# Half-batch 4's k and q: transposed by DMA instead of by TensorE, in a fused attention and SwiGLU kernel

## The chip, the cores and the metric

The kernel runs on one core of a Trainium2 chip. The metric is the device time of one execution in microseconds (us), as the median of several runs. The engines are named as in the profile: PE is TensorE (PEld its weight loads), DVE is VectorE, ACT is ScalarE, POOL is GpSimd, and SP is SyncE, which here only issues transfers.

## The reference

Eight batches of eight heads of causal attention over 576 positions with head size 64, with a bias from a running sum of a score `s`; its output, laid out as 4608 tokens by 512, goes through a SwiGLU block with 1536 hidden channels.

```python
scores = (q @ k.transpose(0, 1, 3, 2)) / np.sqrt(D)
cum = np.cumsum(np.maximum(s, 0.0), axis=-1)
bias = np.minimum(-(cum[:, :, :, None] - cum[:, :, None, :]), 0.0)
scores = np.where(causal, -1e9, scores + bias)
attn = softmax(scores)                       # over the last axis
x = (attn @ v).transpose(0, 2, 1, 3).reshape(B * S, H * D)
g = x @ w_gate
out = (g * sigmoid(g) * (x @ w_val)) @ w_out
```

All inputs and the output are float32; the matrix products inside the kernel are in bfloat16.

## The kernel before

**Units of work.** A half-batch is four heads. There are 16, numbered 0 to 15, and 64 heads, numbered `kk` from 0 to 63; half-batch `h` is `kk // 4` and the head within it is `step`. Before a half-batch can be scored its k and q have to stand transposed (head dimension on the partitions) in one of two buffers, `KQ[hb % 2]`, which has one tile for each pair of rows `r` (0 and 1). Heads with `step` 0 and 1 read the tile of r = 0, heads with `step` 2 and 3 the tile of r = 1.

**The way of k and q.** `load_qk` (L140) brings a half-batch in float32 from DRAM, 576 KB for k and 576 KB for q. `cast_one` makes bfloat16 of them in the tiles `ck` and `cq` (on POOL at L246, later on ACT at L244). From there two ways lead to `KQ`:

- By TensorE: `pe_transpose` (L287) transposes nine 128 by 128 blocks of k and nine of q through the identity matrix into PSUM, in groups of five and four, and `pe_out` copies each group out of PSUM twice, once for each r (ACT at L314 for k, DVE at L316 for q). `prep_one` issues one group; the table `PREP_AT` says when.
- By DMA: `scratch` (L260) writes `ck` and `cq` to DRAM (tiles `ks`, `qs`, 288 KB each), `transposes` (L270) reads them back with a transposing DMA into `pk` and `pq`, and `split` (L274) copies them into `KQ` on DVE, four copies for a half-batch. `scratch` and `transposes` are issued on SP.

The constant `NPE` is the number of half-batches that go by TensorE: 5, so half-batches 0 to 4. Half-batches 5 to 15 go by DMA. `aug` (L183) adds the rows of the bias to `KQ`.

**The order of the work is written out by hand** and the engines follow it, each in its own order. After a start-up part (heads 0 to 7), a generator `attn_items` yields the attention work in pieces, and the loop at the end of the kernel weaves it between the pieces of the SwiGLU block, token tile by token tile (nine tiles of 512 tokens). One head is scored in four pieces (`score_piece`, `ci` 0 to 3, L359 on PE, the exponential at L369 on ACT, masks at L374 and L379 on POOL). `av_piece` (L396) multiplies with V into a PSUM bank, and `av_out` normalises it on DVE (L412, L413) and so frees the bank. For heads 0 to 15 a pair of heads is then transposed by TensorE (`x_pe`, L445) and copied into `XT` on DVE (L452). `XT` is what the gate and value products (L629) read; their results pass ACT (L650) and DVE (L652, L663), and the last product is at L686 or L735.

While half-batch 3 (heads 12 to 15) is scored, the first token tile is in its last product (L686), which holds four of the eight PSUM banks. The other four pass among score pieces, V products and transposes. `take` gives out the bank that was released longest ago, so the bank of every product is fixed when the program is built.

**What else is issued there.** `side` issues loads at given places of the scoring. V of batch 1 is cast on POOL at heads 11 and 12 (L168), and then the five loads of V of batch 2 are issued on SP (`load_v`, L157) into the same buffer; that V is cast on POOL when half-batch 4 is scored. k and q of half-batch 5 are loaded in start-up. Calls of `split` do not run at once: they are put on a list, `later`, and `do_later(1)` takes one of them at places of the loop; in the first token tile past n = 30 it takes none:

```python
if tt == 0 and n > 30:
    pass
elif i >= 2 * NFT or i % (2 if tt == 1 else 4) == 1:
    do_later(1)
```

Whatever of a half-batch is left on the list is taken before its first head is scored.

**SP** works through its list of transfers in order. An instruction that has to wait (for a cast, for the scratch write that a transposing DMA reads, for a free buffer) holds up all that stand behind it. Each transfer also reuses one of eight semaphores in turn, and so waits until the transfer that stands eight places ahead of it has landed.

Of the kernel before, what the change touches and what calls it, by code (L numbers as in the profile page):

```python
# [19 lines left out]
def kernel(  # L20
# [14 lines left out]
    B, H, S, D = q.shape  # L35
# [6 lines left out]
    NHB = BH // HB  # L42
    NR = HB // 2
# [33 lines left out]
        tc.tile_pool(name="dram", bufs=1, space=bass.MemoryType.DRAM)  # L77
    )

    NPE = 5  # L80
    XB = 2
    KS = {i: dram.tile([NR * S, 128], BF16, name=f"ks{i}") for i in range(NPE, NHB)}
    XS = {
        i: dram.tile([NCH * 128, 128], BF16, name=f"xs{i}") for i in range(XB * H // 2, BH // 2)
    }
    QS = {i: dram.tile([NR * S, 128], BF16, name=f"qs{i}") for i in range(NPE, NHB)}

# [16 lines left out]
    first = first_sbuf.enter_context(tc.tile_pool(name="first", bufs=1))  # L104
# [5 lines left out]
    with tc.manual_schedule():  # L110
# [36 lines left out]
        def load_qk(hb):  # L147
            load_one(hb, "k")
            load_one(hb, "q")

        def load_v(b, cs, eng=nc.sync):
            if 0 in cs:
                loaded["v", b] = raw.tile([128, NCH, H, D], FP32, tag="rawv", bufs=1, name="rawv")
            t = loaded["v", b]
            for c in cs:
                n = 128 if c < 4 else TAIL
                eng.dma_start(  # L157
                    t[0:n, c, :, :],
                    v[b, :, c * 128 : c * 128 + n, :].rearrange("h p d -> p h d"),
                )  # L160
# [97 lines left out]
        def scratch(hb):  # L258
            for name, SC in (("k", KS), ("q", QS)):
                nc.sync.dma_start(  # L260
                    SC[hb].rearrange("(x j) c -> x (j c)", j=J),
                    cts[name, hb].rearrange("x j r d -> x (j r d)"),
                )
# [3 lines left out]
        def transposes(hb):  # L267
            for name, SC in (("k", KS), ("q", QS)):
                prs[name, hb] = cp.tile([128, NR * S], BF16, tag="p" + name, bufs=1, name="p" + name)
                nc.sync.dma_start_transpose(prs[name, hb], SC[hb])  # L270
# [184 lines left out]
        later = []  # L455

        def do_later(n):
            while n > 0 and later:
                f, *args = later.pop(0)
                f(*args)  # L460
                n -= 1
# [5 lines left out]
        def side(h, step, ci):  # L467
            bh = HB * h + step
            for c in V1_AT.get((bh, ci), ()):
                cast_v(1, c, nc.gpsimd)  # L470
            if bh == H + 4 and ci == 3:
                load_v(2, range(5))
            if h == 4 and (step, ci) in ((0, 1), (2, 1)):
                load_qk(6 + step // 2)
            if h >= 5 and h + 3 < NHB and (step, ci) == (0, 1):
                load_qk(h + 3)
            hb = h + 1
            if NPE <= hb < NHB:
                late = hb == NPE
                if late and (step, ci) == (0, 1):  # L480
                    scratch(hb)
                if late and (step, ci) == (0, 3):
                    transposes(hb)
                if (step, ci) == (0, 1):
                    aug(hb, GP4)
                first = 1 if hb < NPE + 3 else 0
                if step in (first, first + 1) and ci == (3 if late else 1):
                    for r in range(NR):
                        later.append((split, hb, "kq"[step - first], r))
            hb = h + 2  # L490
            if hb == NPE and step == 3 and ci % 2 == 1:
                cast_one(hb, "kq"[ci // 2], nc.gpsimd)
            if NPE < hb < NHB:
                six = hb == NPE + 1
                if (step, ci) == ((2, 0) if six else (0, 2)):
                    cast_one(hb, "k", nc.scalar)
                if (step, ci) == ((2, 2) if six else (1, 2)):
                    cast_one(hb, "q", nc.scalar)
                if (step, ci) == ((3, 0) if six else (2, 0)):
                    scratch(hb)  # L500
                if (step, ci) == (3, 3 if six else 0):
                    do_later(NR * 2)
                    transposes(hb)
            if ci != 1:
                return
            bn = h // 2 + 1
            if 3 <= bn < B:
                if h % 2 == 0:
                    if step == 2:
                        load_v(bn, (0, 1))  # L510
                    if step == 3:
                        load_v(bn, (2, 3, 4))
# [4 lines left out]
        def side_v(h, step, ci):  # L517
            bn = h // 2 + 1
            if h == 4 and (step, ci) in V2_AT:
                cast_v(2, V2_AT[step, ci], nc.gpsimd)  # L520
            if 3 <= bn < B and h % 2 == 1 and (step, ci) in V_AT:
                cast_v(bn, V_AT[step, ci], nc.scalar)
# [3 lines left out]
        def prep_one(hb, i, eng=None):  # L526
# [7 lines left out]

        PREP_AT = {
            2: {(1, 2): 0, (2, 0): 2, (2, 2): 1, (3, 0): 3},
            3: {(1, 3): 0, (2, 1): 1, (2, 3): 2, (3, 1): 3},
        }

        AV_AT = {  # L540
# [6 lines left out]
        def attn_items():  # L547
            for kk in range(H, BH + 2):
                h, step = divmod(kk, HB)
                if kk < BH:  # L550
                    if step == 0:
                        do_later(NR * 2)
                    if step == 1 and 3 < h + 1 < NPE:
                        cast_one(h + 1, "k", nc.gpsimd)
                        cast_one(h + 1, "q", nc.gpsimd)
                    if step == 2 and 3 < h + 1 < NPE:
                        aug(h + 1, GP4)
                    for ci in range(4):
                        score_piece(kk, ci)
                        side(h, step, ci)  # L560
                        side_v(h, step, ci)
                        yield kk + 0.1 + ci / 8
                        if (step, ci) in PREP_AT.get(h, ()):
                            prep_one(
                                h + 1, PREP_AT[h][step, ci],
                                (nc.scalar, nc.vector)[ci // 2] if h == 2 else None,
                            )
                            yield kk + 0.1 + ci / 8
                for x in X_AT.get(kk, (kk - 2,)):
                    if x % 2 == 1 and H <= x < BH:  # L570
                        if x < XB * H:
                            x_pe(x // 2)
                            yield kk + 0.5
                        else:
                            x_in(x // 2)
                for p in AV_AT.get(kk, (kk - 1,)):
                    if H <= p < BH:
                        av_piece(p, (0, 1, 2))
                        yield kk + 0.6
                        av_piece(p, (3,))  # L580
                        yield kk + 0.7
                        av_piece(p, (4,))
                        av_out(p)
                        if p >= XB * H and p % 2 == 1:
                            x_out(p // 2)
                        yield kk + 0.8
# [369 lines left out]
        aug(3, SP4)  # L956
        load_v(1, range(5))
        load_qk(4)
        load_qk(5)
        x_pe(0, nc.vector)  # L960
        values(4, 5)
        x_pe(1, nc.scalar)
# [40 lines left out]
        for tt in range(NTT):  # L1003
            lo = H * (tt + 1) + LAGS[tt]
            hi = min(H * (tt + 2) + LAGS[tt + 1], BH + 2)
            span = 36 if tt < FIRST7 else 34.5
            if hi == BH + 2:
                span = 30
            n0 = 5 if tt == 0 else 0
            n = 0  # L1010
            todo = {FIRST7 - 1: W_SUMS, FIRST7: W_DIFFS}.get(tt, [])
            if tt == FIRST7:
                for _ in range(3):
                    weight_op(*todo.pop(0))
            for i, cost in enumerate(ffn_items(tt)):
                n += cost
                if todo and (i >= 24 if tt < FIRST7 else i % 2 == 1):
                    weight_op(*todo.pop(0))
                if tt == 0 and n > 30:
                    pass  # L1020
                elif i >= 2 * NFT or i % (2 if tt == 1 else 4) == 1:
                    do_later(1)
                if seconds:
                    seconds.pop(0)()
                for f in hook.pop(n, ()):
                    f()
                done = min(1.0, max(0, n - n0) / (span - n0))
                if tt == 0:
                    done = (
                        0.57 * max(0, n - n0) / (24 - n0) if n < 24  # L1030
                        else min(1.0, 0.57 + 0.43 * (n - 24) / (span - 24))
                    )
                pump(lo + (hi - lo) * done)
# [31 lines left out]
```

## Time and profile before

| what | value |
|---|---|
| median of 3 runs | 376.75 us (376.2 to 377.3) |
| the profiled execution | 375.79 us, of which the span from first to last instruction is 374.0 us |
| PE busy | 360.7 us, 96% of the span |
| DVE, ACT, POOL busy | 289.6 us (77%), 240.4 us (64%), 212.3 us (57%) |
| granted TensorE clock | 0.999 |
| DMA moved | 64.23 MB, mean 172 GB/s |
| SP's queue (hardware dynamic) | 84976 packets, 41.46 MB, 45.2% of 16 engines' span |
| POOL's queue (software dynamic) | 12128 packets, 22.21 MB, 22.6% |

The span counts from the first to the last instruction of the profiled execution; the time counts 1.79 us more that lie around it. All times of day below, such as "at 66.62", are microseconds from the start of that span. A row of the timeline gives start, duration, engine, line, operation, tiles written and read, shapes and how many instructions were merged; in brackets stands the idle time before it and what ended that. Matmuls are pipelined, so a row's duration reaches past the start of the next row on PE: what a group of matmuls costs is the distance between the starts.

### The profile page before, as it was taken

The numbers are of one execution on the slowest core, as the hardware profiler recorded it, in microseconds if no ns is written. First come the engines' busy times: TensorE is split into PE (matmuls) and PEld (weight loads), VectorE is DVE, ScalarE is ACT, GpSimd is POOL, SyncE is SP. The second block draws the span as 40 slices with busy tenths as digits, with TensorE's granted clock in tenths as the row PEclk, the third lists the DMA queues.
The fourth block names the chain that finished last, engine by engine and source line by source line (L and its number), as shares of the span: only waits on it lengthen the run. The fifth ranks groups of instructions, "written<-read, shape, count | busy, mean of one in ns | idle before, by whom it ended". The sixth has DMA issues, their size and how long they took to land.

```text
span 374.0 us, 8759 instructions
## 1 busy us (share of the span) xinstructions
PE 360.7 (96%) x3259; PEld 230.6 (62%) x3300; DVE 289.6 (77%) x578; ACT 240.4 (64%) x471; POOL 212.3 (57%) x325
## 2 busy tenths in 40 slices
PE   7799899999999999999999999999999999999995
PEld 6584456655555556855685559655865585476464
DVE  8968776468995899588967997699858867975984
ACT  8777677698876877588757875686566523323321
POOL 8883555856455647494649464955675516315320
PEclk9999999999999999999999999999999999999999
DMA  7899999799877997896779675984132103002003
GB/s 239 193 258 253 219 257 267 237 303 247 245 186 220 254 262 196 178 281 205 211 167 266 178 182 174 255 206 98 40 119 62 35 19 128 2 0 95 20 0 114
DMA packets 97146, 64.23 MB, mean 172 GB/s; under 512 B 77232, under 2 KB 82736, under 8 KB 97104
## 3 DMA queue, kind: packets, MB, share of 16 engines
q1 hardware_dynamic: 84976, 41.46, 45.2%
q0 software_dynamic: 12128, 22.21, 22.6%
q8 instruction: 26, 0.43, 0.5%
q14 instruction: 16, 0.13, 0.1%
HBM read 37.90 MB, written 19.86 MB: 154 GB/s over the span
## 4 chain that ended last, share of the span: by engine, by line
PE 85%; DMA 6%; POOL 5%; ACT 1%; issue 1%; DVE 1%; DVEq 0%; POOLq 0%; ACTq 0%
PE bank L629 45%; PE bank L735 17%; PE bank L359 10%; PE bank L396 7%; PE bank L686 5%; DMA rawk<-in_k_dram 4%; DMA rawv<-in_v_dram 2%; POOL rawv L157 1%; POOL vt L168 1%; POOL wv L332 1%; ACT pt L369 1%; PE bank L287 0%; POOL rawq L140 0%; ACT kq L314 0%; POOL kq L211 0%
## 5 line engine op out<-in xcount | busy, mean ns | idle before, releaser
L369 ACT ACTIVATE pt<-bank 128x512 bf16<-128x512 f32 (+1 forms) x256 | 120.4, 510 | 31.0 <-PE bank L359 18.2
L629 PE MATMUL bank<-XT,wg 128*128 128x512 bf16 x418 | 110.3, 379 | 1.2 <-DVE pp L652 0.3
L629 PE MATMUL bank<-XT,wv 128*128 128x512 bf16 x412 | 109.3, 379 | 1.1
L650 ACT ACTIVATE th<-bank 128x512 bf16<-128x512 f32 x108 | 64.7, 599 | 55.9 <-PE bank L629 53.6
L652 DVE SCALAR_TENSOR_TENSOR pp<-th,bank 128x512 bf16<-128x512 bf16 x108 | 73.6, 682 | 19.2 <-ACT th L650 18.7
L663 DVE SCALAR_TENSOR_TENSOR ht<-pp,bank 128x512 bf16<-128x512 bf16 x108 | 74.1, 686 | 10.6 <-PE bank L629 0.4
L359 PE MATMUL bank<-kq 128*128 128x128 bf16 (+4 forms) x576 | 75.6, 240 | 1.5 <-DMA kq<-HL 1.0
L672 POOL TENSOR_TENSOR ht<-ht 128x512 bf16<-128x512 bf16 x35 | 40.4, 1154 | 52.2 <-DVE su L670 52.1
L359 PEld LDWEIGHTS <-kq 128*128 128x128 bf16 x576 | 45.8, 98 | 31.5 <-issue 1.9
L629 PEld LDWEIGHTS <-wv 128*128 128x128 bf16 x432 | 38.4, 98 | 36.5 <-issue 0.6
L629 PEld LDWEIGHTS <-wg 128*128 128x128 bf16 x432 | 38.3, 98 | 34.2 <-issue 0.7
L396 PEld LDWEIGHTS <-pt 128*128 128x128 bf16 x960 | 41.9, 98 | 17.2
L374 POOL TENSOR_SCALAR_AFFINE_SELECT pt<-pt 128x512 bf16<-128x512 bf16 x56 | 36.8, 658 | 27.3 <-ACT pt L369 22.7
L396 PE MATMUL bank<-vt,pt 128*128 128x65 bf16 x960 | 47.0, 194 | 0.4 <-POOL vt L168 0.3
L430 POOL DMA_DIRECT2D xs<-ot x24 | 21.7, 905 | 30.0 <-DVE ot L413 27.6
L735 PEld LDWEIGHTS <-ht 128*128 128x128 bf16 x336 | 31.2, 98 | 4.3
L413 DVE TENSOR_TENSOR ot<-bank,rc 128x320 bf16<-128x320 f32 x64 | 31.5, 492 | 2.2
L183 POOL DMA_DIRECT2D kq<-HL x48 | 28.9, 604 | 0.0
L735 PEld LDWEIGHTS <-su 128*128 128x128 bf16 x252 | 23.5, 98 | 3.3
L686 PE MATMUL bank<-wo,ht 128*128 128x512 bf16 x90 | 24.8, 379 | 0.3
L800 POOL TENSOR_TENSOR ysb<-ysb 128x512 f32<-128x512 f32 x12 | 15.2, 1270 | 15.3 <-DVE ysb L794 15.3
L379 POOL TENSOR_SCALAR_AFFINE_SELECT pt<-pt 128x64 bf16<-128x64 bf16 x56 | 14.8, 264 | 15.8 <-ACT pt L369 15.7
(93 smaller groups left out, 384.6 us busy)
## 6 DMA issues: line engine op xcount, KB each, us to landing
out_dram<-ysb POOLq DMA_DIRECT2D x32, 256.0 KB, 4.5
rawv<-in_v_dram SPq DMA_DIRECT2D x28, 256.0 KB
rawk<-in_k_dram SPq DMA_DIRECT2D x12, 576.0 KB
rawq<-in_q_dram SPq DMA_DIRECT2D x12, 576.0 KB
xs<-ot POOLq DMA_DIRECT2D x24, 160.0 KB, 3.5
ks<-ck SPq DMA_DIRECT2D x11, 288.0 KB
qs<-cq SPq DMA_DIRECT2D x11, 288.0 KB
rawk<-in_k_dram POOLq DMA_DIRECT2D x3, 576.0 KB, 7.3
```

The costliest lines, as they stand in the source:

```text
L359: nc.tensor.matmul(sc[:, o : o + w], T[:, 1, e * S + 128 * tj : e * S + 128 * (tj + 1)], T[:, 0, e * S + lo : e * S + hi], start=not maske ...
L369: nc.scalar.activation(pt[:, c0 : c0 + n], sc, AF.Exp, scale=0.125)
L374: nc.gpsimd.affine_select(pt[:, 1088:1600], pt[:, 1088:1600], pattern=[[0, 4], [1, 128]], compare_op=ALU.is_ge, fill=zreg, base=0, channel ...
L396: nc.tensor.matmul(av[:, bi * (D + 1) : (bi + 1) * (D + 1)], pt[:, c0 : c0 + 128], VT[b % 2][:, tj, h, :], start=(tj == 0), stop=(tj == bi),)
L413: nc.vector.tensor_mul(ot[:, :, e * D : (e + 1) * D], av3[:, :, 0:D], rc[:, :, None].to_broadcast([128, NCH, D]),)
L629: nc.tensor.matmul(view(bs, TT), w[:, c, f0 : f0 + 128], xt[:, c, :], start=(c == 0), stop=(c == 3),)
L650: nc.scalar.activation(th, pg, AF.Tanh, scale=0.5)
L652: nc.vector.scalar_tensor_tensor(pp, in0=th, scalar=1.0, in1=pg, op0=ALU.add, op1=ALU.mult)
L663: nc.vector.scalar_tensor_tensor(hp[:, 2 * k2 : 2 * k2 + 2, :].rearrange("p a n -> p (a n)"), in0=pp, scalar=0.5, in1=pv, op0=ALU.mult, op ...
L672: (nc.vector if ft == NFT - 1 else nc.gpsimd).tensor_sub(hp[:, 1:3, :], hp[:, 1:4:2, :], hp[:, 0:3:2, :])
L686: nc.tensor.matmul(view(pys[ts_], DM), hps[ft // 2][:, 2 * (ft % 2) + half, c0 : c0 + 128], WO[j][:, ft % WKO, :], start=(ft == 0), stop=( ...
L735: nc.tensor.matmul(ps, lhs(p), rhs(p), start=(first and p == 0), stop=(last and p == NP - 1), skip_group_check=True,)
```

## The change

Half-batch 4 goes by DMA instead of by TensorE. `NPE` becomes 4, and a new constant `NSC` (5) keeps the places of half-batches 5 and later. While half-batch 3 is scored, `scratch(4)` is placed after the last piece of step 1, `transposes(4)` and the five loads of V of batch 2 after the first piece of step 2, and the four calls of `split` go on the list `later` after the last piece of step 2 (k) and the second piece of step 3 (q). In the first token tile past n = 30 the list is now worked off where its head belongs to half-batch 4. The loads of k and q of half-batch 5 move in the program from start-up to the last score piece of head 12. The casts of half-batch 4 stay on POOL, at their place.

```diff
-    NPE = 5
+    NPE = 4
+    NSC = 5
...
-            if bh == H + 4 and ci == 3:
-                load_v(2, range(5))
+            if h == 3:
+                if (step, ci) == (1, 3):
+                    scratch(4)
+                if (step, ci) == (2, 0):
+                    transposes(4)
+                    load_v(2, range(5))
+                if (step, ci) in ((2, 3), (3, 1)):
+                    for r in range(NR):
+                        later.append((split, 4, "kq"[step - 2], r))
+                if (step, ci) == (0, 3):
+                    load_qk(5)
...
         PREP_AT = {
             2: {(1, 2): 0, (2, 0): 2, (2, 2): 1, (3, 0): 3},
-            3: {(1, 3): 0, (2, 1): 1, (2, 3): 2, (3, 1): 3},
         }
...
-                    if step == 1 and 3 < h + 1 < NPE:
+                    if step == 1 and h == 3:
                         cast_one(h + 1, "k", nc.gpsimd)
                         cast_one(h + 1, "q", nc.gpsimd)
-                    if step == 2 and 3 < h + 1 < NPE:
+                    if step == 2 and h == 3:
                         aug(h + 1, GP4)
...
         load_qk(4)
-        load_qk(5)
...
                 if tt == 0 and n > 30:
-                    pass
+                    if later and later[0][1] == 4:
+                        do_later(1)
```

In the lines left out `NPE` is replaced by `NSC` in `side`, where the places of half-batches 5 and later are worked out.

More of the change, by code (lines that the diff above doesn't have):

```diff
@@ L477, in side @@
             hb = h + 1
-            if NPE <= hb < NHB:
-                late = hb == NPE
+            if NSC <= hb < NHB:
+                late = hb == NSC
                 if late and (step, ci) == (0, 1):
@@ L485, in side @@
                     aug(hb, GP4)
-                first = 1 if hb < NPE + 3 else 0
+                first = 1 if hb < NSC + 3 else 0
                 if step in (first, first + 1) and ci == (3 if late else 1):
@@ L490, in side @@
             hb = h + 2
-            if hb == NPE and step == 3 and ci % 2 == 1:
+            if hb == NSC and step == 3 and ci % 2 == 1:
                 cast_one(hb, "kq"[ci // 2], nc.gpsimd)
-            if NPE < hb < NHB:
-                six = hb == NPE + 1
+            if NSC < hb < NHB:
+                six = hb == NSC + 1
                 if (step, ci) == ((2, 0) if six else (0, 2)):
```

## The prediction

> **What bounds the kernel now.** I read the chain of waits first.
>
> ```profile
> PE 85%; DMA 6%; POOL 5%; ACT 1%; issue 1%; DVE 1%; DVEq 0%; POOLq 0%; ACTq 0%
> ```
>
> PE sets the time, and outside start-up it hardly rests, so a microsecond taken from PE's queue or put into it as a wait moves the end by a microsecond. Then the timeline of PE where half-batch 3 is scored.
>
> ```profile
> 57.58 0.44 PE L287 MATMUL bank<-ident,ck 128*128 128x128 bf16 x5
> 57.86 0.44 PE L445 MATMUL bank<-ident,ot 128*128 128x128 bf16 x5
> ...
> 61.43 0.44 PE L287 MATMUL bank<-ident,cq 128*128 128x128 bf16 x5
> 61.71 0.38 PE L359 MATMUL bank<-kq 128*128 128x320 bf16 x2
> ...
> 66.40 0.39 PE L287 MATMUL bank<-ident,cq 128*128 128x128 bf16 x4
> 66.62 0.38 PE L359 MATMUL bank<-kq 128*128 128x320 bf16 x2
> ...
> 68.90 0.39 PE L359 MATMUL bank<-kq 128*128 128x128 bf16 x4
> ```
>
> No row has idle time before it. The L287 rows are the transposes that go away; the row at 68.90 is the first of half-batch 4's scores, the deadline of its k and q. Third, SP's timeline.
>
> ```profile
> 54.18 9.56 SPq L157 DMA_DIRECT2D rawv<-in_v_dram  x5
> 63.85 0.55 SPq L140 DMA_DIRECT2D rawk<-in_k_dram  x1
> 64.50 0.42 SPq L140 DMA_DIRECT2D rawq<-in_q_dram  x1
> 68.21 0.36 SPq L260 DMA_DIRECT2D ks<-ck  x1
> 69.49 0.35 SPq L260 DMA_DIRECT2D qs<-cq  x1
> 71.14 1.74 SPq L270 DMA_TRANSPOSE pk<-ks  x1
> 72.98 1.29 SPq L270 DMA_TRANSPOSE pq<-qs  x1
> ```
>
> That is half-batch 5's way by DMA, the model for half-batch 4's. Its landings, from the trace's semaphore records: ks 71.1, qs 72.0, pk 75.6, pq 77.5; ahead of them k of 5 at 59.8, q of 5 at 61.6, V of batch 2 from 62.4 to 66.8, k and q of 6 at 68.7 and 70.3. Last, DVE's timeline, which shows when the copies out of pk are due.
>
> ```profile
> 63.60 0.46 DVE L452 COPY XT<-bank 128x576 bf16<-128x576 bf16 x1
> 64.47 0.20 DVE L412 RECIPROCAL rc<-bank 128x5 f32<-128x5 f32 x1 [0.41 <-PE bank L396]
> 64.70 0.49 DVE L413 TENSOR_TENSOR ot<-bank,rc 128x320 bf16<-128x320 f32 x1
> ...
> 79.58 0.45 DVE L274 COPY kq<-pk 64x1152 bf16<-64x1152 bf16 x1
> 79.95 0.67 DVE L652 SCALAR_TENSOR_TENSOR pp<-th,bank 128x512 bf16<-128x512 bf16 x1
> ```
>
> Half-batch 5's first copy runs at 79.58, 4.0 us after pk landed. Keep that margin in mind.
>
> **What goes away.** 18 transposes on PE. By the distance of starts the four groups take 0.28 (57.58 to 57.86), 0.28 (61.43 to 61.71), 0.23 (62.60 to 62.83) and 0.22 (66.40 to 66.62): 1.01 us, all on the path. Four ACT copies (1.51 + 1.47 us) and four DVE copies (1.66 + 1.46) go too; PE waited for none of them, so they are worth nothing. Added on DVE are four splits of 0.45 to 0.95 us, less than what leaves it: nothing by themselves, but for their waits.
>
> **What does not move.** The loads of half-batch 5 change place in the program, but the order of the built instructions shows them in the same place on SP, straight behind those of 4, with the same waits. SP does not wait for PE, so they start at 45.59 as before: nothing. The casts of 4 keep their place on POOL (54.30 and 56.88, the second held by the landing of q of 4 at 56.8).
>
> **The new chain, step by step.** SP issues the scratch writes behind the casts, at 55.4 and 58.0. Their data stand behind k and q of 5 in the same rings. In the row of before a scratch write landed 0.8 us after the load ahead of it (70.3 to 71.1), so ks of 4 lands at 61.6 + 0.8 = 62.4 and qs 0.9 later. SP waits for ks, issues pk (1.74 us) and then pq. The latency from issue to landing was 4.4 us for pk of 5 and 4.5 for pq: pk lands at 66.8, pq, issued at 64.3, at 68.8. Over all 22 such transposes the latency was 3.0 to 7.9 us, the long ones with loads of V ahead; I take 4.4, since here too only small transfers stand ahead. The earliest is 61.6 + 3.0 = 64.6, the latest I allow 62.4 + 6.4 = 68.8, 6.4 being that of pk of 6.
>
> [...]
>
> **The first wait.** By the order of DVE's instructions the first split of k stands behind the XT copy of heads 10 and 11 (63.60) and ahead of the normalising of heads 12 and 13 (64.47, 65.51). DVE gets there at 63.0, since its old copies are gone and PE is earlier, and stands still until 66.8. Then 0.45 for the split and 0.62 for the normalising (64.47 to about 65.1): head 12's V bank is free at 67.9. PE needs that bank for the third score piece of head 15; before, that was the row at 66.62, now due at 66.62 - 1.01 = 65.6. So PE waits 2.3 us. Behind it the second split and head 13's normalising (69.0) feed the fourth piece and the transposes of heads 12 and 13 and cost about 0.1 more; q's first split, after pq at 68.8, is done at 69.5, ahead of the first scores of half-batch 4 at about 70.3 against 68.90 before. Net of the 1.01 saved, +1.4. PE loses nothing here if pk lands by 64.4, and breaks even at about 65.4.
>
> **The second wait.** The five V loads now stand behind pq on SP and are issued from 65.6 instead of 54.18. Everything behind keeps its distance, but now starts from pq's landing (68.8) and not from that of q of 5 (61.6): 7.2 us later. V of batch 2 lands at 69.6 to 74.0, and POOL casts it from 74.38 + 1.4: in time. k and q of 6 land at 75.9 and 77.5; ACT casts them at 76.51 + 1.4 and 79.75 + 1.4: in time, by 2 us. ks of 5 lands at 78.3, pk of 5 is issued then and lands at 82.8 with 4.4 to 4.5. DVE wants it at 79.58 + 1.4 = 81.0. The margin of 4.0 us is used up and DVE waits 1.8. There DVE runs with hardly a gap, and PE's next uses of the banks that DVE frees have little room (the V bank normalised by about 83.9 is taken by the value product at 84.07), so all but 0.2 reaches PE: +1.6. pq of 5 lands at 84.7, due 87.4: in time. At half-batch 6 pk landed 0.5 us before its copy (93.3 and 93.77). SP was idle for 3.7 us before (75.50 to 79.17), so that much of the 7.2 is absorbed; 3.5 remains against a slip of 3.0: just in time, 0 to 0.3.
>
> **Sum.** -1.01 + 2.4 + 1.6 = +3.0. From the profiled execution, 374.0 of span and 1.79 around it, that is 375.79 + 3.0 = 378.8; the median of the runs lies 0.96 above that execution, so 376.75 + 3.0, about 379.7. With pk of 4 at 65.9 to 68.5 and the queue moving with it, the likeliest case alone gives 377.9 to 381.9.
>
> **Rivals.** *No wait (chance 0.2).* The rings drain faster without V in them, ks lands with q of 5 and pk takes 3.0: landing at 64.6, pq soon after, and half-batch 5 then moves by some 5 us, pk landing at about 79.4. PE keeps nearly all of its 1.01 us: 375.8. For it: the shortest latencies in the profile (3.0, 3.1). Against: those have nothing ahead of them in the queue. It decides at pk of 4 by 64.4 and pk of 5 by 79.8. *First wait only (0.15).* pk of 4 late, but V and the loads of 6 go faster in a queue with no tail of 5 in it, so that pk of 5 lands by 81: 376.75 + 1.4 = 378.1, with an early pk 377.3. *The delay runs on (0.1).* Output stores on POOL's queue (256 KB each, four issued from 73.14 to 79.07) now share the engines with the scratch writes of 5; at the 6.4 us latency pk of 5 lands at 84.7 or later, half-batch 6 and the XT transposes behind it are late as well: +5 to +7, 382 to 384. The forecast holds 0.55.
>
> A run tells about 0.3% (1.1 us) from no change: 375.6 to 377.9 is "same". The no-wait rival lies near the lower edge and gives 0.1 faster, 0.1 same; the first-wait rival gives 0.05 same, 0.1 slower; the rest is slower. The range runs from the no-wait rival's time to the likeliest case's upper end: 375.7 to 381.9, leaving out faster runs below it and most of the running-on case.
>
> **What would show it.** In the changed kernel's profile: no L287 rows near 58 to 67; the loads of 5 still issued at about 45.6; DVE idle 3 to 4 us ahead of an L274 row near 66.8, released by pk; PE idle about 2 us before a score piece, released by DVE's normalising; V of batch 2 issued from about 65.6; a second idle time of DVE ahead of L274 near 81 to 83. Wrong would be: pk landing by 64.4, or PE finding its banks free in spite of a waiting DVE.

## The result, and the profile after

Five executions of the changed kernel took 378.12 to 381.78 us, median 380.77, beside five of the kernel before with a median of 376.2: a ratio of 1.0113 (95% interval 1.0078 to 1.0148). In a second series the same kernel took 377.63 to 381.44, median 378.23 of eight, beside 376.11: 1.0065 (1.0033 to 1.0098). The change costs 2.1 to 4.6 us; it gains nothing.

Two executions of it were profiled. I call them the first (378.12 us, span 376.3) and the second (377.63 us, span 375.4). Each is the fastest of its series. The chain of waits of the first:

```profile
PE 81%; DMA 8%; SPq 5%; POOL 2%; DVE 1%; ACT 1%; issue 1%; DVEq 0%; POOLq 0%
```

The 5% of SP's queue are loads of V in start-up (25.7 to 42.6), where the chain takes another way in each of the three profiles, so they are not the change. What the change puts into the chain is half-batch 4's way by DMA: the scratch write of its k from 55.55 (6.29 us), the transposing DMA from 61.90 (3.45 us) and the work on DVE behind it, up to 67.97.

SP's timeline of the first profile shows half-batch 4's way by DMA, V of batch 2 behind it, and half-batch 5's way behind that:

```profile
55.55 0.36 SPq L261 DMA_DIRECT2D ks<-ck  x1
58.00 0.35 SPq L261 DMA_DIRECT2D qs<-cq  x1
61.90 1.30 SPq L271 DMA_TRANSPOSE pk<-ks  x1
63.31 1.30 SPq L271 DMA_TRANSPOSE pq<-qs  x1
64.66 4.50 SPq L158 DMA_DIRECT2D rawv<-in_v_dram  x5
...
70.42 0.42 SPq L261 DMA_DIRECT2D ks<-ck  x1
70.92 0.38 SPq L261 DMA_DIRECT2D qs<-cq  x1
77.13 1.31 SPq L271 DMA_TRANSPOSE pk<-ks  x1
```

Half-batch 5's scratch write of k was issued at 68.21 before and is now at 70.42, only 2.2 us later. But SP stands from 70.92 + 0.38 to 77.13 until that write has landed, which took 2.9 us before and takes 6.7 now, while V of batch 2 (landed by 73.3) and the loads of 6 (76.4) are still under way ahead of it. By the trace's semaphore records pk of 5 landed at 75.6 before, at 81.5 in the first profile and at 80.7 in the second.

DVE's timeline of the second profile, where half-batch 4's copies run:

```profile
65.00 0.45 DVE L275 COPY kq<-pk 64x1152 bf16<-64x1152 bf16 x1 [2.26 <-DMA pk<-ks]
65.37 0.18 DVE L413 RECIPROCAL rc<-bank 128x5 f32<-128x5 f32 x1
65.59 0.49 DVE L414 TENSOR_TENSOR ot<-bank,rc 128x320 bf16<-128x320 f32 x1
66.11 1.36 DVE L275 COPY kq<-pk 64x1152 bf16<-64x1152 bf16 x1
67.50 0.20 DVE L413 RECIPROCAL rc<-bank 128x5 f32<-128x5 f32 x1
67.73 0.49 DVE L414 TENSOR_TENSOR ot<-bank,rc 128x320 bf16<-128x320 f32 x1
...
80.76 0.45 DVE L275 COPY kq<-pk 64x1152 bf16<-64x1152 bf16 x1 [0.30 <-DMA pk<-ks]
...
96.57 0.45 DVE L275 COPY kq<-pk 64x1152 bf16<-64x1152 bf16 x1 [1.53 <-DMA pk<-ks]
```

DVE stands 2.26 us for pk of 4 and only then normalises heads 12 and 13 (L413, L414). PE, in the same profile, stands for these two normalisings, ahead of the third and fourth score pieces of head 15:

```profile
65.15 0.38 PE L360 MATMUL bank<-kq 128*128 128x448 bf16 x2
66.13 0.38 PE L360 MATMUL bank<-kq 128*128 128x320 bf16 x2 [0.59 <-DVE ot L414]
66.35 0.81 PE L695 MATMUL bank<-wo,ht 128*128 128x512 bf16 x3
68.28 0.19 PE L360 MATMUL bank<-kq 128*128 128x64 bf16 x1 [1.12 <-DVE ot L414]
```

In the profile of before the row between them stood at 66.62, and none had idle time before it:

```profile
66.18 0.38 PE L359 MATMUL bank<-kq 128*128 128x448 bf16 x2
...
66.84 0.81 PE L686 MATMUL bank<-wo,ht 128*128 128x512 bf16 x3
67.49 0.19 PE L359 MATMUL bank<-kq 128*128 128x64 bf16 x1
```

In the first profile the two gaps are 1.52 and 0.42. A gap counts from the end of the row ahead, which reaches 0.16 past the next start (0.38 against 0.22), so PE's loss is read from the starts. From the start of the second score piece of head 15 to that of the fourth, 1.31 us passed before, of which 0.22 were transposes, so 1.09 without them; it is 3.13 in the second profile (65.15 to 68.28) and 3.35 in the first (64.66 to 68.01). The first wait cost PE 2.04 and 2.26 us. What PE's queue gained and lost, from the starts of equal matmuls in the profiles of before and after:

| stretch | first | second |
|---|---|---|
| ahead of it, at 54 | -0.73 | -0.24 |
| 54 to 66: three of the four groups of transposes gone | -0.79 | -0.79 |
| 66 to 71: the fourth group, the first wait, and the clock | +3.64 | +1.82 |
| 71 to 86: the second wait | 0 | +0.39 |
| half-batch 6, about 97 | +0.34 | +0.31 |
| to the end | +0.14 | +0.14 |
| PE's delay at the end | +2.60 | +1.63 |

The first row is the start-up, which differs between executions of one kernel by about a microsecond. The 1.82 of the second profile are the 2.04 of the wait less 0.22 for the last transposes. The 3.64 of the first are 2.26 less 0.22, and 1.60 of something that the prediction did not have. This is a table of stretches of the first profile; PEclk is the granted clock:

```profile
core 0: us, PE busy (x) PEld busy (x) DVE busy (x) ACT busy (x) POOL busy (x), PEclk, DMA share, GB/s
64.56:67.97 3.41, 1.51 (x9) 0.66 (x7) 2.47 (x7) 1.51 (x3) 1.95 (x2) 1.00 1.04 217
67.97:71.39 3.42, 3.38 (x29) 2.40 (x29) 2.04 (x5) 0.23 (x2) 1.33 (x2) 0.50 1.31 215
```

After the stretch in which PE rested for 1.90 us, its clock was halved for 3.42 us. PE was busy throughout, and what took 2.92 us before (67.49 to 70.41) took 4.52 (68.01 to 72.53). In the second profile the clock stayed at 1.00.

### The profile page after: what moved, and what is told of

The parts are those of the page before. It is cut to its first block, busy times and chain, and to the rows that moved or that the text cites. A ratio compares the mean times of both kernels' runs of the same rounds, so it can differ in the third digit from the quotient of the medians.

```text
span 376.3 us, 8765 instructions
## 1 busy us (share of the span) xinstructions
PE 364.8 (97%) x3282; PEld 231.5 (62%) x3282; DVE 288.2 (77%) x578; ACT 237.7 (63%) x467; POOL 213.0 (57%) x325
## 4 chain that ended last, share of the span: by engine, by line
PE 81%; DMA 8%; SPq 5%; POOL 2%; DVE 1%; ACT 1%; issue 1%; DVEq 0%; POOLq 0%
PE bank L638 43%; PE bank L744 17%; PE bank L360 10%; PE bank L397 6%; SPq L158 5%; PE bank L695 4%; DMA rawk<-in_k_dram 3%; DMA pk<-ks 2%; DMA ks<-ck 2%; ACT pt L370 1%; DMA kq<-HL 1%; PE bank L354 1%; DVE kq L275 0%; DVE pp L661 0%; POOL kq L215 0%
## 5 line engine op out<-in xcount | busy, mean ns | idle before, releaser
L638 PE MATMUL bank<-XT,wv 128*128 128x512 bf16 x432 | 110.9, 379 | 0.1
L414 DVE TENSOR_TENSOR ot<-bank,rc 128x320 bf16<-128x320 f32 x64 | 31.5, 491 | 2.2
L695 PE MATMUL bank<-wo,ht 128*128 128x512 bf16 x96 | 26.6, 388 | 0.0
```

The source lines that it names most:

```text
L414: nc.vector.tensor_mul(ot[:, :, e * D : (e + 1) * D], av3[:, :, 0:D], rc[:, :, None].to_broadcast([128, NCH, D]),)
L638: nc.tensor.matmul(view(bs, TT), w[:, c, f0 : f0 + 128], xt[:, c, :], start=(c == 0), stop=(c == 3),)
L695: nc.tensor.matmul(view(pys[ts_], DM), hps[ft // 2][:, 2 * (ft % 2) + half, c0 : c0 + 128], WO[j][:, ft % WKO, :], start=(ft == 0), stop=( ...
```

## The experiments

Every kernel was compared with the kernel before on the same chip; its median there was 376.11 us for the first four runs below, 375.61 for the next four and 375.69 for the last four.

**The changed kernel again.**

> The changed kernel, unaltered, for the profile of another execution. In the profile shown, the kernel took 378.12 us, the fastest of its five times; the median is 380.77, so some 2.6 us of the loss lie in something that this profile doesn't show. Theory (the waits vary with the DMA's landings): where an execution takes 380 to 382 us, keys of half-batch 4 land later than 65.3 (up to the predicted 66.8), PE's wait before head 15's second score piece is 2.4 us or more, and PE waits again for half-batch 5's transposed keys at 81 to 83. Rival (the clock): the landings stay within 0.3 us of those shown, and the stretch at a granted clock of 0.50 that follows PE's wait is longer than 3.4 us, or comes twice.

Median 378.23. The second profile above is of this run. It is no slower execution, so it does not answer what the executions of 380 to 382 us held: three of the five in the first series and one of the eight here. The keys of 4 landed at 65.0 (not later than 65.3, as the theory had it), and the clock did not fall (as the rival had it). What it shows instead is the second wait, small, where the first profile has none.

**Leaving the transposing out: what can be gained.**

```diff
-            3: {(1, 3): 0, (2, 1): 1, (2, 3): 2, (3, 1): 3},
```

> The kernel before, without transposing half-batch 4's keys and queries at all: heads 16 to 19 take half-batch 2's in their place, at no cost in time, and nothing is put on the DMA queues instead. This is the most that the change could gain. Theory (PE sets the end, and its 1.01 us come through): 375.4 us in the state of the runs shown, 0.7 to 1.1 faster than the kernel before. Rival (DMA is nearly as late as PE in this stretch, and half-batch 6's keys land 0.5 us ahead of their use): 0.3 to 0.6 us faster, the rest turned into a wait for keys at 93 to 97 us.

374.32 us, ratio 0.9948 (0.9930 to 0.9966): 1.8 us faster than before, with an interval of 1.3 to 2.6, more than the 0.7 to 1.1 that was forecast. In its profile PE's delay goes from -1.01 at 54 to -2.01 at 68 and stays there. The 1.0 us of PE comes through whole; the other 0.8 of the median no profile explains; pk of 5 landed at 75.1 and nobody waited for it.

**The first wait taken away.** The splits of 4 stand behind the normalising on DVE.

```diff
-                if (step, ci) in ((2, 3), (3, 1)):
-                    for r in range(NR):
-                        later.append((split, 4, "kq"[step - 2], r))
+                if step == 3 and ci < 3:
+                    split(4, "kkq"[ci], ci % 2)
+                if (step, ci) == (3, 3):
+                    later.append((split, 4, "q", 1))
...
-                    if later and later[0][1] == 4:
-                        do_later(1)
+                    pass
```

> The changed kernel, with the additions that split half-batch 4's transposed keys and queries moved behind head 15's score pieces on VectorE, so that nothing that PE needs stands behind a wait for the transposes. Theory (the first wait costs 1.5 us of idling and, by the lower clock that follows it, 1.6 more; the shifted SP queue is a second cost that comes due when PE is early): PE's idle time of 1.5 us before head 15's second score piece goes, the granted clock stays at 1.0 to 75 us, PE reaches half-batch 5's first scores 3 us earlier, and then waits there about 2.5 us for keys that land at 81.5 as before: 0 to 1.5 us faster than the changed kernel, 0.5 to 2 slower than the kernel before, with the lower clock perhaps moved to 82. Rival (the first wait is the whole cost): 4 us faster than the changed kernel, 1 us faster than the kernel before.

379.29 us, ratio 1.0102 (1.0064 to 1.0141): 1.1 us slower than the changed kernel, though the two intervals overlap, where the theory had 0 to 1.5 faster and the rival 4 faster. The first wait is gone: PE's delay stays between -0.3 and 0.0 from 63 to 80. Then DVE and PE stand for half-batch 5:

```profile
83.58 0.45 DVE L275 COPY kq<-pk 64x1152 bf16<-64x1152 bf16 x1 [3.90 <-DMA pk<-ks]
```

```profile
84.68 1.02 PE L639 MATMUL bank<-XT,wv 128*128 128x512 bf16 x4 [2.80 <-DVE pp L662]
```

The expectation had this wait, but the landing at 81.5 and not at 83.6. This execution was later by 1.5 us at 54 than the first profile, and half-batch 4's scratch writes by 1.9 to 2.1.

**The first wait filled.** 30 products that nobody reads, ahead of head 15's second score piece.

```diff
             sc = view(bs, n)
+            if (bh, ci) == (15, 1):
+                for _ in range(30):
+                    nc.tensor.matmul(sc[:, 0:128], ident, ident, start=True, stop=True)
```

> The changed kernel, with 30 products of 128 columns that nobody uses put on PE ahead of head 15's second score piece, in the bank that this piece overwrites; they take some 1.6 us, and PE stood idle for 1.5 us a little later in any case. Theory (the granted clock of 0.50 from 68.0 to 71.4 follows from PE's idling): PE is busy through the wait for VectorE, the clock stays at 1.0, and the kernel is 1 to 1.7 us faster than the changed one. Rival (the clock follows from something else, or the products delay the bank that they take): the clock falls as before, and the kernel is 0 to 1.6 us slower than the changed one.

378.69 us, against 378.23 for the changed kernel beside it: no gain. The clock stayed at 1.00, but it had stayed there in the second profile of the changed kernel too, so the run does not show that idling halves it. What it shows is again the other wait: with 0.42 us of idling left at 67.58, PE was 0.09 behind at 80 and stood 1.63 us for DVE, which had waited 2.71 for pk of 5, landed at 82.4.

**The traffic alone.** The kernel before, with half-batch 4's stores and DMA transposes beside it.

```diff
-            if bh == H + 4 and ci == 3:
+            if bh == H + 5 and ci == 3:
+                scratch(4)
+            if bh == H + 6 and ci == 0:
+                transposes(4)
                 load_v(2, range(5))
```

> The kernel before with all its transposes on PE, and beside them, as traffic that nobody reads, the scratch stores and DMA transposes of half-batch 4, with V 2 behind them on SP as in the changed kernel. Nobody waits for half-batch 4's transposes, so the first wait can't come; PE saves nothing either. Theory now (the landing of half-batch 5's transposed keys sets the time: in the four runs of the changed kind PE's delay after that stage, against the kernel before, was that landing less 79.0 to 79.6 us): they land at 80.7 to 83.6 here too, PE waits for them, and the kernel is 1.4 to 4 us slower than before, as slow as the changed one. Rival (the prediction's sum, in which both waits count one after the other): without the first wait, and with the second at 1.6, it is 1.6 us slower than before and 1.4 faster than the changed kernel if that is 3 us slower.

378.12 us, ratio 1.0083 (1.0053 to 1.0112), which is 2.0 to 4.2 us: the 1.6 of the rival lies outside, and it is as slow as the changed kernel. Nothing on PE or DVE waits for half-batch 4 here.

```profile
81.31 0.45 DVE L274 COPY kq<-pk 64x1152 bf16<-64x1152 bf16 x1 [2.08 <-DMA pk<-ks]
```

This is the clearest of the runs. The loss of the change is there without its first wait. Over the profiles, the start of this copy less 79.58, its start before, is PE's delay behind the stage:

| kernel | first copy of 5 starts | less 79.58 | PE's delay at 86 | released by |
|---|---|---|---|---|
| changed, second profile | 80.76 | 1.18 | 1.18 | pk of 5 |
| traffic alone | 81.31 | 1.73 | 1.74 | pk of 5 |
| first wait filled | 82.47 | 2.89 | 2.90 | pk of 5 |
| first wait taken away | 83.58 | 4.00 | 4.00 | pk of 5 |
| changed, first profile | 81.70 | 2.12 | 2.12 | DVE's own queue, 0.2 us after pk of 5 landed |

So the two waits are not a sum. pk of 5 sets a floor for the delay, and what PE loses before it comes off what it loses there. Why pk of 5 lands anywhere from 80.7 to 83.6 in these profiles no run parts; its scratch write took 6.2 to 7.8 us and the transposing DMA 3.7 to 5.4.

**V of batch 2 back in its old place**, ahead of half-batch 4's stores.

```diff
+            if bh == H + 4 and ci == 3:
+                load_v(2, range(5))
...
                     transposes(4)
-                    load_v(2, range(5))
```

> The changed kernel with the five loads of V 2 back in their old place, ahead of half-batch 4's scratch stores on SP; all else as changed. Theory (what SP holds ahead of a transpose sets its landing): V 2's fifth load goes out at 63.7 in the kernel before, so the scratch stores go out at about 64 instead of 56 to 58, half-batch 4's keys land at 72 to 73 instead of 65, and VectorE stands until then: PE waits 6 to 8 us more at head 15, 4 to 6 us slower than the changed kernel; half-batch 5's keys then land late for nobody. Rival (DMA work, not its order, sets the time): the same as the changed kernel within 1 us.

383.94 us, ratio 1.0225 (1.0199 to 1.0252), 8.3 more than before, where the changed kernel had 2.1 and 4.6 more in its two series. As the theory had it, pk of 4 landed at 72.1 and PE stood:

```profile
73.22 0.58 PE L360 MATMUL bank<-kq 128*128 128x320 bf16 x2 [7.77 <-DVE ot L414]
```

With half-batch 4 on SP, V has to stand behind its transposes.

**The loads of half-batch 6 behind half-batch 5's transposes.**

```diff
-            if h == 4 and (step, ci) in ((0, 1), (2, 1)):
-                load_qk(6 + step // 2)
+            if h == 4 and (step, ci) == (2, 1):
+                load_qk(7)
...
                     transposes(hb)
+                    load_qk(6)
```

> The changed kernel with one step moved: the loads of half-batch 6 go out on SP behind half-batch 5's two DMA transposes instead of ahead of its scratch stores. Theory (half-batch 5's transposed keys set the time): its scratch stores go out 1.2 us earlier and are not behind 1.2 MB of loads, so they land 2 to 3 us earlier and the transposed keys at 77.5 to 79 instead of 80.7 to 81.5; the second wait goes, the first wait (1.7 to 1.9 us of PE) then counts whole, and the kernel is 0.5 to 1.5 us faster than the changed one and 0.5 to 1.5 slower than before. Rival (the first wait sets the time, the second only fills what it leaves): no difference to the changed kernel. A third: half-batch 6's loads are late for the casts on ScalarE at 81 to 85, and the kernel is slower by 1 to 3 us.

381.97 us, ratio 1.0166 (1.0143 to 1.0190). pk of 5 landed at 78.5, as expected, and its copy waited for nothing of DMA. The third theory came true instead, though its 1 to 3 us were too few: ACT stood for the k of 6, ahead of work that PE needs, and PE's delay went from 0.70 at 80 to 5.5 at 86. Part of that is the clock, at 0.50 from 84.25 to 87.66.

```profile
82.00 1.15 ACT L245 CAST ck<-rawk 128x1152 bf16<-128x1152 f32 x1 [4.68 <-DMA rawk<-in_k_dram]
```

**An attempt at a faster version**: the splits later, the loads of 6 behind as above, and two of V's five loads between the stores and the transposes of 4.

```diff
                     scratch(4)
+                    load_v(2, range(2))
                 if (step, ci) == (2, 0):
                     transposes(4)
-                    load_v(2, range(5))
+                    load_v(2, range(2, 5))
...
```

> The changed kernel with three steps moved, an attempt at a version faster than both: the splits of half-batch 4 behind head 15's normalising on VectorE; V 2's first two loads between half-batch 4's scratch stores and its transposes, where the DMA engines were half idle; half-batch 6's loads behind half-batch 5's transposes. Theory (one wait in each place, and each comes from the order on its queue): neither wait comes, PE's 1.0 us come through as in the kernel that leaves the transposes out, and it is 0.5 to 1.2 us faster than before. Rival (DMA has too little room between 55 and 98 us for the added 1.2 MB, whatever the order): a wait comes up later, at half-batch 6's transposed keys at 93 to 98 us, and the kernel is 0 to 2 us slower than before.

380.15 us, ratio 1.0114 (1.0082 to 1.0145), 4.5 us slower than before; neither forecast holds. pk of 5 landed at 76.1, but V's loads put pk of 4 back from 65.0 to 66.2, the splits ran up to half-batch 4's first scores (PE idle 1.51 us at 69.40), and ACT stood 1.90 us for the k of 6. No kernel that keeps half-batch 4's DMA was faster than before. For three more versions, and for the kernel without half-batch 4's transposing with V moved, all with DMA transposes, there is no time: only the keys by DMA; the same with the splits and the queries of 6 later; and this version with the loads of 6 in their old place.

**Plain DMAs in place of DMA transposes.** Four kernels in which every DMA transpose is a plain DMA of the same bytes, at the same place of the same queue.

```diff
-                nc.sync.dma_start_transpose(prs[name, hb], SC[hb])
+                nc.sync.dma_start(prs[name, hb], SC[hb].rearrange("(x j) c -> x (j c)", x=128))
...
-                nc.sync.dma_start_transpose(XT[:, r, at : at + hi - lo], XS[pr][lo:hi])
+                nc.sync.dma_start(XT[:, r, at : at + hi - lo],
+                    XS[pr][lo:hi].rearrange("r c -> (r c)").rearrange("(p m) -> p m", p=128))
```

> The kernel before, in which every DMA transpose is replaced by a plain DMA of the same bytes from the same scratch, on the same queue at the same place: keys, queries and XT are left untransposed, the rest is as before. It is the ground for the next three, and tells what a DMA transpose takes beside a plain DMA in this kernel (half-batch 5's keys: 4.4 us from issue to landing in the kernel before). Theory (the transposes take the DMA engines longer than their bytes do): the same transfer takes 2.5 to 3.5 us, half-batch 5's keys land 1 to 2 us earlier, and the time is within 1 us of the kernel before, as PE waits for none of them there. Rival (they take as long as plain DMAs, behind the same queues): 4 to 4.5 us.

> The changed kernel with the same replacement of every DMA transpose by a plain DMA of the same bytes (keys, queries and XT left untransposed). Theory (the chain store, landing, issue on SP and V 2 ahead of half-batch 5 make the delay, whatever the second transfer is): half-batch 5's keys land 4 to 6 us later than in the ground kernel of this kind, PE waits at 79 to 83, and it is 1 to 2.5 us slower than that ground. Rival (the DMA transposes' own work on the engines is what delays the queue): the keys land in time, and it is as fast as the ground or 1 us faster.

> The kernel without any transposing for half-batch 4 (heads 16 to 19 take half-batch 2's keys and queries), again with plain DMAs for every DMA transpose left. The same 1.0 us of PE as with the transposes: 0.8 to 1.8 us faster than its ground, no wait; the rival, that half-batch 5's keys are then late for PE, would give less than 0.5.

> The last kernel with V 2's loads where the changed kernel has them: the move of V 2 without the added DMA, plain DMAs for every DMA transpose left. Theory A (the order: V 2's 1.2 MB closer ahead of half-batch 5's stores is most of the delay): half-batch 5's keys land 3 us or more later than without the move, and half or more of the changed kernel's delay in this kind of kernel is there. Theory B (the added stores and reads back are most of it): they land less than 2 us later, and the time is that without the move within 0.5 us.

The ground took 375.84 us (ratio to before 0.9996, 0.9970 to 1.0021), the changed kernel of this kind 376.07 (1.0002, 0.9976 to 1.0028), the one without transposing 375.04 and the one with V moved 374.41. The last two differ by nothing and so part nothing: without half-batch 4's transfers on SP there is nothing that V's loads could be put behind, so both have the same instructions in the same order on every engine. Their 0.6 us apart is what two medians of one program differ by. In both profiles PE gains 1.0 us from 54 to 68, as with the DMA transposes.

SP's timeline of the changed kernel with plain DMAs, against the one above:

```profile
61.53 0.32 SPq L271 DMA_DIRECT2D pk<-ks  x1
62.25 0.32 SPq L271 DMA_DIRECT2D pq<-qs  x1
62.62 5.25 SPq L158 DMA_DIRECT2D rawv<-in_v_dram  x5
```

A plain DMA held SP for 0.32 us here, a transposing one for 1.30; pk of 5 took 3.1 us to land in the plain ground and 4.4 in the kernel before. V goes out 2.0 us earlier. Counted from the end of the issue, pk of 5 landed after 2.8 us in the plain ground (3.11 - 0.32) and 2.7 in the kernel before (4.44 - 1.74); over all 22 such transfers the medians are 3.0 and 2.6. So what a transposing DMA takes longer here is its issue. In the changed kernel with plain DMAs pk of 5 landed 4.5 us later than in its ground, as the theory had it, but at 79.2, and the copy started at 79.76 without a wait:

```profile
79.76 0.45 DVE L278 COPY kq<-pk 64x1152 bf16<-64x1152 bf16 x1
```

PE kept the first wait (0.50 and 1.21 us idle) and no second, and the kernel is 0.2 us from its ground, with some 1.4 us of uncertainty, where I expected 1 to 2.5. From 54 to 86 PE's delay against the ground grew by 1.0 in these two profiles, all of it at the first wait. For the second wait the rival was nearer: the time that the transposing DMAs add on SP turns the last of the margin into a wait.

## Why the prediction was right, and where it was not

- *PE saves 1.01 us.* Right: 0.79 by 66, the rest after, and 1.00 in the kernel without the transposing.
- *The loads of 5 do not move.* Right: 45.41 and 45.92, against 45.59.
- *pk of 4 lands at 66.8.* It landed at 65.3 and 65.0. ks was 0.6 to 0.8 us earlier (61.8 and 61.6 for 62.4) and the latency, taken from pk of 5 as 4.4, was 3.4 and 3.3, while the DMA engines were half idle from 60 to 64 (DMA share 0.49 and 0.54, against 0.91 before).
- *The first wait costs 2.4 us.* The place and the releaser were right, and it cost 2.26 and 2.04. Its terms were not, and their errors nearly cancel: DVE waited less, 3.12 and 2.26 instead of 3.8, but the step "cost about 0.1 more" for the second split was too small. That split ran beside a cast on POOL and took 0.66 and 1.36 us, and the gap behind it was 0.42 and 1.12.
- *Half-batch 5 moves by 7.2 us, pk of 5 at 82.8, due at 81.0.* It moved by 5.9 and 5.1, to 81.5 and 80.7, for the most part since pq of 4 landed at 66.7 and 66.1 instead of 68.8. In the first profile pk of 5 was just in time, because the half clock had made PE later; in the second it cost 0.39. By its stated sign the second profile is the first-wait-only rival (pk of 5 "by 81", 378.1 us; it was 80.7, and the median 378.23), with only those 0.39 against it. The runs with the first wait away show that the second stands behind it: the sum was built rightly, as a landing against a time due that the first wait had already moved, but it made the first wait look like 1.4 us of the loss. Taking that wait away brought nothing.
- *Half-batch 6, 0 to 0.3.* 0.34 and 0.31.
- *The sum.* +3.0 was forecast; -1.01 + 2.26 + 1.60 + 0.34 + 0.14 = +3.3 in the first profile, and -1.01 + 2.04 + 0.39 + 0.31 + 0.14 = +1.9 in the second. That the first comes so near is luck: 1.60 of it is the half clock, which took the place of the second wait. The medians, 4.6 and 2.1 above before, lie on both sides of the forecast, and the 2.6 us that the first has over its profiled execution no profile shows.
- *TensorE or DMA for half-batch 4.* 1.0 us on PE stood against a delay of 5.1 to 5.9 us on SP's queue, where the margin was 4.0. From the end of the issue a transposing DMA of pk of 5 took as long as a plain one (2.7 us against 2.8 for the same bytes); from its start it did not, 4.4 against 3.1, since the issue held SP for 1.74 us against 0.32.

Not settled: how much of half-batch 5's 5 to 6 us V's move makes and how much the added transfers; and why three of the five executions of the first series took 380 to 382 us. None of these was profiled, their mean clock was 0.991 to 0.996, and in the second series an execution of 381.44 us had a clock of 1.00.

## What to carry to other kernels

The transfers added to SP's queue were paid for by what stood behind them (pk of 5 landed 5.1 and 5.9 us later): look for the first landing behind it with a small margin (here 4.0 us for the next half-batch's keys) and price the change there. When two waits lie in line, test which one is the floor by adding the traffic without the consumer; removing the visible wait alone can bring nothing. The loads of 6, moved back on SP, freed what was behind them (pk of 5 landed at 78.5 instead of 80.7 and 81.5) and were late themselves, so that ACT waited 4.68 us: the consumer of what moves back needs a margin too.

## What the runs showed of the hardware

- **The clock was halved for 3.42 us in the first profile, and the longest gap does not tell when it falls.** It stood at 0.50 from 67.97 there, where the longest gap of that stage was 1.52; for 6.8 us (69.4 to 76.2) with V in its old place, where PE stood for 7.77; and from 84.25 to 87.66 with the loads of 6 behind, where PE stood for 3.40. With the first wait taken away, one gap of 2.80 left it at 1.00:

```profile
80.26:83.67 3.41, 1.62 (x26) 1.02 (x23) 0.09 (x1) 1.98 (x4) 0.23 (x1) 1.00 1.14 241
```

  In these 3.41 us PE was busy for 1.62 and kept its clock; in the first profile it was busy for 1.51 of the 3.41 us ahead of the half clock. What decides is not shown by these runs.
- **Four splits on DVE that started beside a cast on POOL ended 0.3 us after the cast**: one took 1.36 us instead of 0.45. POOL's timeline of the second profile has, beside DVE's row at 66.11,

```profile
66.01 1.14 POOL L247 CAST ck<-rawk 128x1152 bf16<-128x1152 f32 x1
```

  The split ends at 67.47, 0.32 after the cast; the three other splits of the two profiles that started beside a cast took 0.66, 0.85 and 1.10 us and ended 0.31 or 0.32 after it. Where a split was the first to start (65.37 in the first profile), the cast beside it, at 65.52, took 1.36 us instead of 1.14. The runs do not show why.
